# The order of attention units and output steps on TensorE, changed in a fused attention and FFN kernel

## The chip, the core and the metric

The kernel runs on one core of a Trainium2 chip. The metric is the device time of one execution in microseconds (us). Three runs of the kernel before gave 245.78, 246.03 and 246.22 us, so the median is 246.03 us. The execution that the profiler recorded took 245.78 us; its span, from the first to the last instruction of the program, is 244.0 us, so 1.78 us lie outside the span.

## The reference

Inputs are `q`, `k`, `v` of shape (4, 8, 768, 64), a small matrix `sort_net` (4, 8, 8, 8), and FFN weights `w_a`, `w_b` (512 x 1536) and `w_out` (1536 x 512). What is computed, cut to the core:

```python
P = sort_net
for _ in range(5):                       # rows, then columns, sum to one
    P = exp(P - P.max(-1)); P /= P.sum(-1); P /= P.sum(-2)
k_s = einsum('bhij,bhjcd->bhicd', P, k_b)    # k and v: 8 blocks of 96 rows, mixed by P
v_s = einsum('bhij,bhjcd->bhicd', P, v_b)
attn = softmax(q_b @ k_s.T / sqrt(64))       # within each block
x = concat_heads(attn @ v_s)                 # 3072 x 512
out = ((x @ w_a) * (x @ w_b)) @ w_out        # 3072 x 512
```

## The kernel before, in words

There are 4 batches with 8 heads each. Two heads are a **pair**; pairs are counted through, g = 0 to 15, four to a batch (`HP` = 4). The FFN of batch b runs on TensorE while the attention of batch b+1 is put in small pieces between the FFN's steps. Everything on TensorE (PE), GpSimd (POOL) and the SyncE queue (SP) runs in the order in which the Python code issues it (`manual_schedule`, L399). After the opening part, the order on VectorE (DVE) and ScalarE (ACT) is chosen by the scheduler.

**FFN steps.** `ffn_ab(b, m, t)` (L340) makes 128 of the 1536 hidden rows for half a batch: 4 matmuls for a and 4 for b (L332, 384 columns each, into the PSUM pool `psF`), a copy of a to SBUF by ACT (L352), and the product a*b by DVE into `hT` (L353). There are 24 such steps to a batch; for batch 0 the 12 steps with t = 0 run earlier, so 12 are left. `ffn_out(b, c)` (L368) makes 128 output rows: 12 accumulating matmuls of 512 columns (L377) into `po`, a copy to `o_sb` by ACT for even c and by DVE for odd c (`store`, L384), and the DMA to `out` on the SP queue. In the kernel before, `ffn_out` gives two steps of 6 matmuls each. There are 6 outputs c to a batch; I call them po0 to po5, and their halves po0a, po0b.

**Attention units.** A pair g of batch 1 to 3 has three units (L530):

- C, `c_(g)`: for g < 7 a transpose of q on TensorE (`turn_q`, L255); 12 matmuls that mix k and 12 that mix v (`stage_mix`, L274, L281), each into its own tile of `psA`; ACT copies k to `kT` in two copies and the second half of v to `vT`, DVE copies the first half of v. For g > 4 a DMA transpose on SP turns `vT` into `vs` (L292). From g = 6 a tiny POOL copy waits for `kT` (the gate, L539), and the loads of pair g+2 follow it.
- S, `s_(g)`: 16 matmuls of scores (`stage_scores`, L295, L302), 8 for each half of the blocks, each half into a tile of `psA`, and an exponential by ACT for each half (L307). Its weights are `kT`, its moving data the transposed q (`qT`). From g = 7 to 14 it also issues the next pair's q repack on POOL (`pair_q`, L244) and the DMA transpose on SP (`stage_q`, L250).
- O, `o_(g)`: 16 matmuls `o_ps` (L231) in two halves, each into a tile of `psA`; DVE takes reciprocals (L235) and scales into `xp` (L237); a DMA transpose on SP writes `xT` (L318), which the next batch's FFN reads.

The pool `psA` has two tiles of two PSUM banks, taken in turn. So the first half of an S or O needs the tile that the first half of the unit before it used to be read out, and the second half the other one. `psF` has four tiles of one bank. `kT`, `vT`, `vs` and `eT` have three buffers each, taken by g modulo 3.

**The order.** `paced` (L570) goes through the FFN's steps and puts in as many units after each as keeps the two in proportion. With C0 for the first pair of the coming batch, and "ab" for one `ffn_ab` step, the order during batch 0 is

```
ab C0 ab S0 ab ab C1 ab S1 ab ab C2 ab O0 ab ab S2 ab C3 ab po0a O1 po0b S3
po1a po1b O2 po2a O3 po2b po3a po3b po4a po4b po5a po5b
```

and during batches 1 and 2

```
ab C0 ab ab S0 ab ab ab C1 ab ab ab S1 ab ab C2 ab ab ab O0 ab ab ab S2 ab ab C3
ab ab ab O1 ab ab po0a S3 po0b po1a O2 po1b po2a po2b O3 po3a ... po5b
```

**The opening.** P is normalized, and the first half of batch 0's attention runs in pairs (`half_mix`, `half_scores`, `half_v`, `half_o`, `half_x`). Then five FFN accumulations are begun ahead of their last summand (`begun`, L488): three in `psF`, and two in the first halves of two `psA` tiles named `two` (L489). The steps ffn_ab(0,0,0), (0,1,0) and (0,2,0) add the last summand to them: the second step finishes begun 3, the third begun 4.

Of the kernel before, what the change touches and what calls it, by code (L numbers as in the profile page):

```python
# [9 lines left out]
FP32 = mybir.dt.float32  # L10
# [6 lines left out]
def _ap(t: bass.AP, extra_offset, pattern):  # L17
    return bass.AP(tensor=t.tensor, offset=t.offset + extra_offset,
                   ap=[list(p) for p in pattern])
# [3 lines left out]
def kernel(  # L23
# [11 lines left out]
    nc = tc.nc  # L35
    P = 128
    B, H, S, D = q.shape
# [3 lines left out]
    DMODEL = H * D  # L41
# [4 lines left out]
    NCH = S // P  # L46
    HP = H // 2
    KA = DMODEL // P
    KO = DFF // P
# [17 lines left out]
    psA = ctx.enter_context(tc.tile_pool(name="psA", bufs=2, space=PSUM))  # L67
    psF = ctx.enter_context(tc.tile_pool(name="psF", bufs=4, space=PSUM))
# [19 lines left out]
    def load_pair(b, hp):  # L88
        tiles = []
        for name, t in (("k2", k), ("v2", v), ("q2", q)):  # L90
            base = (b * H + 2 * hp) * S * D
            if b == 0 and name == "q2":
                continue
            to = ld.tile([P, 2, W], BF16, tag=name, name=name)
            nc.gpsimd.dma_start(out=to, in_=_ap(t, base, [[W, P], [S * D, 2], [1, W]]))  # L95
            tiles.append(to)
        loaded[b * HP + hp] = tiles
# [3 lines left out]
    w_out_sb = const.tile([P, KO, DMODEL], BF16, name="w_out_sb")  # L101
# [42 lines left out]
    def xT_of(b):  # L144
        if b not in xTs:
            xTs[b] = xtp.tile([P, KA, S], BF16, tag="xT", name="xT")
        return xTs[b]
# [12 lines left out]
    def copy(eng, out, in_):  # L160
        if eng == "act":
            nc.scalar.copy(out=out, in_=in_)  # L162
        else:
            nc.vector.tensor_copy(out=out, in_=in_)  # L164
# [79 lines left out]
    def pair_q(g):  # L244
        qc = qtp.tile([P, NCH, 2, D], BF16, tag="qc", name="qc", bufs=4)
        nc.gpsimd.tensor_copy(out=qc.rearrange("p c e d -> p e c d"),  # L246
                              in_=loaded[g][2].rearrange("p e (c d) -> p e c d", c=NCH))
        st[g, "qc"] = qc

    def stage_q(g):  # L250
        qT = qtp.tile([P, NCH, P], BF16, tag="qTf", name="qTf", bufs=4)
        nc.sync.dma_start_transpose(out=qT, in_=st[g, "qc"].rearrange("p c e d -> p (c e d)"))
        st[g, "qT"] = qT

    def turn_q(g, eng="dve"):  # L255
        q2 = loaded[g][2] if g >= HP else q_first[:, 2 * g:2 * g + 2]
        q_ps = psF.tile([P, NCH, P], BF16, tag="F", name="q_ps")
        for c in range(NCH):
            for e in range(2):
                nc.tensor.matmul(q_ps[e * D:(e + 1) * D, c, :],  # L260
                                 lhsT=q2[:, e, c * D:(c + 1) * D],
                                 rhs=ident, is_transpose=True)
        qT = qtp.tile([P, NCH, P], BF16, tag="qT", name="qT")
        copy(eng, qT, q_ps)
        st[g, "qT"] = qT

    def turn_v(g):
        vT, vs = vTs[g % NBUF], vss[g % NBUF]
        vs_ps = psF.tile([P, NB, P], BF16, tag="F", name="vs_ps")
        for i in range(NB):  # L270
            nc.tensor.matmul(vs_ps[:, i], lhsT=vT[:, i], rhs=ident, is_transpose=True)
        nc.vector.tensor_copy(out=vs[0:BLK, :, V0:V0 + P], in_=vs_ps[0:BLK])
# [43 lines left out]
    def to_xT(g):  # L316
        xT, xp = xT_of(g // HP), st[g, "xp"]
        nc.sync.dma_start_transpose(  # L318
            out=xT[:, g % HP, :].rearrange("p (i t) -> p i t", i=NB),
            in_=xp.rearrange("p i e d -> p (i e d)"))  # L320


    hTs = {}
# [32 lines left out]
    def ffn_last(b, c):  # L356
        hT = hTs[b]
        rows = out[b * S:(b + 1) * S, :].rearrange("(p c) n -> c p n", c=NCH)
        for n0, n1, eng, queue in ((0, 384, "act", nc.sync), (384, DMODEL, "dve", nc.scalar)):
            po = psF.tile([P, 512], FP32, tag="F", name="po")  # L360
            for m in range(KO):
                nc.tensor.matmul(po[:, 0:n1 - n0], lhsT=hT[:, m, c * P:(c + 1) * P],  # L362
                                 rhs=w_out_sb[:, m, n0:n1], start=(m == 0), stop=(m == KO - 1))
            o_sb = ffp.tile([P, 512], FP32, tag="o_sb", name="o_sb", bufs=3)
            copy(eng, o_sb[:, 0:n1 - n0], po[:, 0:n1 - n0])
            queue.dma_start(out=rows[c][:, n0:n1], in_=o_sb[:, 0:n1 - n0])

    def ffn_out(b, c):  # L368
        if b == B - 1 and c == NCH - 1:
            return [lambda: ffn_last(b, c)]  # L370
        held = {}

        def part(n):
            if n == 0:
                held["po"] = psF.tile([P, DMODEL], FP32, tag="F", name="po")
            for m in range(n * KO // 2, (n + 1) * KO // 2):
                nc.tensor.matmul(held["po"], lhsT=hTs[b][:, m, c * P:(c + 1) * P],  # L377
                                 rhs=w_out_sb[:, m, :], start=(m == 0), stop=(m == KO - 1))
            if n == 1:
                store(b, c, held["po"])  # L380

        return [lambda: part(0), lambda: part(1)]

    def store(b, c, po):  # L384
        o_sb = ffp.tile([P, DMODEL], FP32, tag="o_sb", name="o_sb", bufs=3)
        copy("act" if c % 2 == 0 else "dve", o_sb, po)
        if b == 0:
            h, u = divmod(c, 3)
            for c2 in range(2):
                nc.sync.dma_start(  # L390
                    out=_ap(out, (h * PH * NCH + 2 * u + c2) * DMODEL,
                            [[NCH * DMODEL, PH], [1, DMODEL]]),
                    in_=o_sb[c2 * PH:(c2 + 1) * PH])
        else:
            rows = out[b * S:(b + 1) * S, :].rearrange("(p c) n -> c p n", c=NCH)
            nc.sync.dma_start(out=rows[c], in_=o_sb)


    with tc.manual_schedule(engines={ET.PE, ET.Pool, ET.SP}):  # L399
        with tc.manual_schedule(engines={ET.Activation, ET.DVE}):  # L400
# [7 lines left out]
            for it in range(5):  # L408
# [15 lines left out]
                if it > 0:  # L424
                    nc.tensor.matmul(heat[0:NB, 1, 0:NB], lhsT=rsum, rhs=rsum,
                                     start=True, stop=True)
# [59 lines left out]
            half_x(0, 2, "act")  # L486
            half_o(0, 3)
            begun = [psF.tile([P, 512], FP32, tag="F", name="pf") for _ in range(3)]  # L488
            begun += [psA.tile([P, 2, 512], FP32, tag="A", name="two")[:, 0] for _ in range(2)]  # L489
            for n, (m, w_sb) in enumerate(((0, w_a_sb), (0, w_b_sb), (1, w_a_sb),  # L490
                                           (1, w_b_sb), (2, w_a_sb))):
                if n == 3:
# [37 lines left out]
        def units_full(b):  # L530
            g0, us = b * HP, []

            def c_(g):
                if g < 2 * HP - 1:
                    turn_q(g)
                stage_mix(g, "k", ("act",))
                stage_mix(g, "v", ("dve", "act"))
                if 2 * HP - 2 <= g < B * HP - 2:
                    nc.gpsimd.tensor_copy(out=gate, in_=kTs[g % NBUF][0:1, 0:1])  # L539
                    load_pair((g + 2) // HP, (g + 2) % HP)  # L540

            def s_(g):
                stage_scores(g)
                if g == HP:
                    turn_v(g)
                if g == HP + 1:
                    stage_q(2 * HP - 1)
                if 2 * HP <= g + 1 < B * HP:
                    pair_q(g + 1)
                    stage_q(g + 1)  # L550

            def o_(g):
                stage_o(g)
                to_xT(g)

            for u, n in ((c_, 0), (s_, 0), (c_, 1), (s_, 1), (c_, 2), (o_, 0), (s_, 2), (c_, 3),
                         (o_, 1), (s_, 3), (o_, 2), (o_, 3)):
                us.append(lambda u=u, g=g0 + n: u(g))
            return us

        def interleave(steps, units, spare, slow=0):
# [6 lines left out]
                    done += 1  # L568

        def paced(ab, po, units, spare):  # L570
            steps = ab + po
            total = len(steps) - 2 * spare
            done = 0
            for now, step in enumerate(steps, 1):
                step()
                while done < len(units) and done * total < now * len(units):
                    units[done]()
                    done += 1

        steps = [lambda: ffn_ab(0, 0, 0, begun[0:2]), lambda: ffn_ab(0, 1, 0, begun[2:4]),  # L580
                 lambda: ffn_ab(0, 2, 0, begun[4:5])]
# [3 lines left out]
        for b in range(B):  # L585
            ab = [lambda m=m, t=t, b=b: ffn_ab(b, m, t)
                  for m in range(KO) for t in range(2) if b > 0 or t == 1]
            po = [f for c in range(NCH) for f in ffn_out(b, c)]
            paced(ab, po, units_full(b + 1) if b + 1 < B else [], 3 if b == 0 else 2)


# [28 lines left out]
```

## Time and profile before

| what | value |
| --- | --- |
| three runs | 245.78, 246.03, 246.22 us; median 246.03 us |
| profiled execution | 245.78 us, span 244.0 us |
| TensorE matmul busy | 236.7 us, 97% of the span |
| VectorE, ScalarE, GpSimd busy | 109.6 us (45%), 104.6 us (43%), 60.6 us (25%) |
| matmuls of L332 (768) | start to start 162.5 ns in a run of them |
| matmuls of L377 (276) | start to start 216 ns in a run of them |
| TensorE clock granted | 1.00 throughout |
| batch 0 with its units, from C0 on | 45.50 to 85.04 us |
| batch 1 with its units | 85.04 to 139.56 us: 54.52 us |
| batch 2 with its units | 139.56 to 194.08 us: 54.52 us |
| batch 3, no units | 194.08 to 243.97 us |

The profile of one execution is read in views: the busy time of each engine, groups of instructions by source line with their mean duration, the chain of work that ended last, the timeline of instructions, and the time from a DMA's issue to its landing. A matmul's listed duration (326 ns for 384 columns) overlaps the next matmul, so the time that a row of matmuls takes is read from start to start. "Idle before, releaser" names what an engine waited for.

### The profile page before, as it was taken

How to read it: one execution, taken by the hardware profiler on the slowest of the kernel's cores; microseconds unless marked ns; L12 is line 12 of the kernel's file. 1: busy time of each engine (PE TensorE's matmuls, PEld its weight loads, DVE VectorE, ACT ScalarE, POOL GpSimd, SP SyncE). 2: the span in 40 equal slices, each digit the busy share in tenths (PEclk: the TensorE clock that was granted, in tenths of full speed). 3: DMA queues.
4: the chain of work that ended last, by engine and by line, in shares of the span. 5: the costliest groups of instructions: out<-in, count | busy, mean ns of one | idle time of the engine just before them, and what ended most of it. 6: DMA issues, size and time to landing. Idle time of an engine off the chain costs nothing.

```text
span 244.0 us, 5508 instructions
## 1 busy us (share of the span) xinstructions
PE 236.7 (97%) x2246; PEld 137.3 (56%) x2258; DVE 109.6 (45%) x259; ACT 104.6 (43%) x204; POOL 60.6 (25%) x87
## 2 busy tenths in 40 slices
PE   7889999999999999999999999999999999999995
PEld 2466666666545466666654466666654466665443
DVE  6774566555536144464625144454524243443110
ACT  3665864466730065646440065646430133333001
POOL 8875577613230043240500053200000000000000
PEclk9999999999999999999999999999999999999999
DMA  5999999958998659987783449924243310000122
GB/s 80 202 199 197 197 200 201 206 84 81 172 157 183 138 100 127 160 135 84 110 140 119 121 95 126 169 46 66 43 79 118 118 46 0 0 3 1 43 112 103
DMA packets 53129, 27.82 MB, mean 114 GB/s; under 512 B 29936, under 2 KB 50160, under 8 KB 53104
## 3 DMA queue, kind: packets, MB, share of 16 engines
q0 software_dynamic: 20944, 14.16, 40.6%
q1 hardware_dynamic: 32016, 13.25, 28.9%
q8 instruction: 17, 0.28, 0.5%
q14 instruction: 8, 0.07, 0.1%
q10 hardware_dynamic: 144, 0.07, 0.1%
HBM read 28.32 MB, written 6.29 MB: 142 GB/s over the span
## 4 chain that ended last, share of the span: by engine, by line
PE 94%; DVE 3%; issue 1%; ACT 1%
PE pf L332 52%; PE po L377 24%; PE mix L281 4%; PE o_ps L231 3%; PE sc L302 2%; PE heat L168 2%; PE mixh L180 2%; PE po L362 1%; PE vs_ps L208 1%; PE sc L195 1%; PE xt_ps L222 1%; PE q_ps L260 1%; PE two L332 1%; DVE xp L237 1%; DVE o_sb L164 0%
## 5 line engine op out<-in xcount | busy, mean ns | idle before, releaser
L353 DVE TENSOR_TENSOR hT<-a_sb,pf 128x384 bf16<-128x384 bf16 x95 | 52.6, 553 | 73.8 <-PE pf L332 47.1
L332 PE MATMUL pf<-xT,w_a_sb 128*128 128x384 bf16 x380 | 77.9, 326 | 0.0
L332 PE MATMUL pf<-xT,w_b_sb 128*128 128x384 bf16 x380 | 77.4, 326 | 0.0
L352 ACT CAST a_sb<-pf 128x384 bf16<-128x384 f32 x95 | 45.5, 479 | 60.9 <-PE pf L332 41.3
L377 PE MATMUL po<-w_out_sb,hT 128*128 128x512 bf16 x265 | 61.3, 379 | 0.6
L332 PEld LDWEIGHTS <-w_b_sb 128*128 128x128 bf16 x384 | 37.5, 98 | 24.6
L332 PEld LDWEIGHTS <-w_a_sb 128*128 128x128 bf16 x384 | 34.9, 98 | 22.3
L377 PEld LDWEIGHTS <-hT 128*128 128x128 bf16 x276 | 26.3, 98 | 30.0
L162 ACT COPY o_sb<-po 128x512 f32<-128x512 f32 (+1 forms) x13 | 7.5, 578 | 46.8 <-PE po L377 45.2
L164 DVE COPY o_sb<-po 128x512 f32<-128x512 f32 (+1 forms) x12 | 7.9, 655 | 35.2 <-PE po L377 26.3
L307 ACT ACTIVATE eT<-sc 96x768 bf16<-96x768 f32 x24 | 18.1, 802 | 6.8 <-PE sc L302 6.8
L539 POOL COPY gate<-kT 1x1 bf16<-1x1 bf16 x8 | 1.4, 179 | 76.1 <-ACT kT L162 76.1
L237 DVE TENSOR_TENSOR xp<-o_ps,rec 96x512 bf16<-96x512 f32 x24 | 15.9, 684 | 0.4
L162 ACT CAST kT<-mix 128x384 bf16<-128x384 f32 x24 | 10.3, 482 | 8.3 <-PE mix L281 8.3
L95 POOL DMA_DIRECT2D k<-in_k_dram x16 | 11.6, 724 | 5.1 <-PE pf L332 2.0
L95 POOL DMA_DIRECT2D v<-in_v_dram x16 | 11.5, 722 | 2.3 <-PE pf L332 0.7
L231 PEld LDWEIGHTS <-eT 96*128 96x128 bf16 x256 | 10.3, 97 | 3.2 <-DVE xp L237 0.6
L235 DVE RECIPROCAL rec<-o_ps 96x8 f32<-96x8 f32 x32 | 5.6, 189 | 14.0 <-PE o_ps L231 14.0
L231 PE MATMUL o_ps<-vs,eT 96*128 96x65 bf16 x256 | 11.3, 193 | 0.2 <-DVE xp L237 0.2
L246 POOL COPY qc<-q 128x768 bf16<-128x768 bf16 x9 | 7.6, 845 | 7.8 <-DMA q<-in_q_dram 7.8
L95 POOL DMA_DIRECT2D q<-in_q_dram x12 | 8.7, 722 | 1.6 <-DMA w_a_sb<-in_moe_w_a_dram 0.7
L168 PE MATMUL heat<-warm 128*128 128x512 bf16 x20 | 7.1, 497 | 1.4 <-DVE warm L77 1.3
(80 smaller groups left out, 155.4 us busy)
## 6 DMA issues: line engine op xcount, KB each, us to landing
out_dram<-o_sb SPq DMA_DIRECT2D x17, 256.0 KB, 2.0
k<-in_k_dram POOLq DMA_DIRECT2D x16, 192.0 KB, 5.3
v<-in_v_dram POOLq DMA_DIRECT2D x16, 192.0 KB, 6.9
q<-in_q_dram POOLq DMA_DIRECT2D x12, 192.0 KB, 7.1
w_a_sb<-in_moe_w_a_dram POOLq DMA_DIRECT2D x6, 256.0 KB, 10.5
w_b_sb<-in_moe_w_b_dram POOLq DMA_DIRECT2D x6, 256.0 KB, 10.2
w_out_sb<-in_moe_w_out_dram POOLq DMA_DIRECT2D x3, 512.0 KB, 10.0
out_dram<-o_sb SPq DMA_DIRECT2D x12, 128.0 KB, 2.4
```

The source lines that it names most:

```text
L95: nc.gpsimd.dma_start(out=to, in_=_ap(t, base, [[W, P], [S * D, 2], [1, W]]))
L162: nc.scalar.copy(out=out, in_=in_)
L164: nc.vector.tensor_copy(out=out, in_=in_)
L168: nc.tensor.matmul(ps[:, 0:cols], lhsT=warm[:, 0:P], rhs=warm[:, 0:cols], start=True, stop=True)
L231: nc.tensor.matmul(o_ps[:, e, i * (D + 1):(i + 1) * (D + 1)], lhsT=eT[:, hf, e, i * BLK:i * BLK + P], rhs=vs[0:BLK, i0 + i, V0 - 1 + e * ( ...
L237: nc.vector.tensor_tensor(out=_ap(xp, i0 * 2 * D, [[nxp * 2 * D, BLK], [D, 2], [2 * D, NBH], [1, D]]), in0=_ap(o_ps, 1, [[1024, BLK], [511 ...
L281: nc.tensor.matmul(mix[e * D:(e + 1) * D, c // 3, c % 3 * P:(c % 3 + 1) * P], lhsT=src2[:, e, c * D:(c + 1) * D], rhs=s_all[:, 2 * g + e], ...
L307: nc.scalar.activation(out=eT[:, hf, :, 0:HB], in_=sc[0:BLK, :, 0:HB], func=AF.Exp, scale=float(scale))
L332: nc.tensor.matmul(pf[:, 0:HW], lhsT=w_sb[:, kc, m * P:(m + 1) * P], rhs=x_cols(b, kc, t), start=(kc == 0), stop=(kc == KA - 1))
L352: nc.scalar.copy(out=a_sb, in_=pf[:, 0:HW])
L353: nc.vector.tensor_mul(out=hT[:, m, t * HW:(t + 1) * HW], in0=a_sb, in1=ab[1][:, 0:HW])
L377: nc.tensor.matmul(held["po"], lhsT=hTs[b][:, m, c * P:(c + 1) * P], rhs=w_out_sb[:, m, :], start=(m == 0), stop=(m == KO - 1))
```

## The change

The diff, cut to its core:

```diff
     def ffn_out(b, c):
-        held = {}
-        def part(n):
-            if n == 0:
-                held["po"] = psF.tile([P, DMODEL], FP32, tag="F", name="po")
-            for m in range(n * KO // 2, (n + 1) * KO // 2):
-                nc.tensor.matmul(held["po"], ...
-            if n == 1:
-                store(b, c, held["po"])
-        return [lambda: part(0), lambda: part(1)]
+        po = psF.tile([P, DMODEL], FP32, tag="F", name="po")
+        for m in range(KO):
+            nc.tensor.matmul(po, ...
...
-            begun += [psA.tile([P, 2, 512], FP32, tag="A", name="two")[:, 0] for _ in range(2)]
+            two = psA.tile([P, 2, 512], FP32, tag="A", name="two")
+            begun += [two[:, 0], two[:, 1]]
...
             def s_(g):
-                if 2 * HP <= g + 1 < B * HP:
-                    pair_q(g + 1)
-                    stage_q(g + 1)
             def o_(g):
                 stage_o(g)
                 to_xT(g)
+                if 2 * HP <= g + 2 < B * HP:
+                    pair_q(g + 2)
+                    stage_q(g + 2)
-            for u, n in ((c_, 0), (s_, 0), (c_, 1), (s_, 1), (c_, 2), (o_, 0), (s_, 2), (c_, 3),
-                         (o_, 1), (s_, 3), (o_, 2), (o_, 3)):
-                us.append(lambda u=u, g=g0 + n: u(g))
+            for n in range(HP + 1):
+                if n < HP:
+                    us.append(lambda g=g0 + n: c_(g))
+                    us.append(lambda g=g0 + n: s_(g))
+                if n > 0:
+                    us.append(lambda g=g0 + n - 1: o_(g))
...
         def paced(ab, po, units, spare):
-            steps = ab + po
-            total = len(steps) - 2 * spare
+            steps = [(1, f) for f in ab] + [(2, f) for f in po]
+            total = sum(t for t, f in steps) - 2 * spare
```

No instruction is added or dropped. The units come in the order C0 S0 C1 S1 O0 C2 S2 O1 C3 S3 O2 O3, an output step is one piece of 12 matmuls that counts double in the pacing, q's repack and transpose for pair g+2 are issued in the unit O of pair g, and begun 3 and 4 share one `psA` tile. Written out, the order during batch 0 becomes

```
ab C0 ab S0 ab ab C1 ab S1 ab ab O0 ab C2 ab ab S2 ab O1 ab po0 C3 S3
po1 O2 po2 O3 po3 po4 po5
```

and during batches 1 and 2

```
ab C0 ab ab S0 ab ab ab C1 ab ab ab S1 ab ab O0 ab ab ab C2 ab ab ab S2 ab ab O1
ab ab ab C3 ab ab po0 S3 po1 O2 po2 O3 po3 po4 po5
```

On ACT the scheduler puts the copy of po0 to `o_sb` in batch 0 ahead of the three copies of C3. On SP the DMA transpose of `vs` for C3 follows the stores of po0, as it follows the `xT` of O1.

More of the change, by code (lines that the diff above doesn't have):

```diff
@@ L369, in ffn_out @@
         if b == B - 1 and c == NCH - 1:
-            return [lambda: ffn_last(b, c)]
-        held = {}
-        def part(n):
-            if n == 0:
-                held["po"] = psF.tile([P, DMODEL], FP32, tag="F", name="po")
-            for m in range(n * KO // 2, (n + 1) * KO // 2):
-                nc.tensor.matmul(held["po"], lhsT=hTs[b][:, m, c * P:(c + 1) * P],
-                                 rhs=w_out_sb[:, m, :], start=(m == 0), stop=(m == KO - 1))
-            if n == 1:
-                store(b, c, held["po"])
-        return [lambda: part(0), lambda: part(1)]
-    def store(b, c, po):
+            ffn_last(b, c)
+            return
+        hT = hTs[b]
+        po = psF.tile([P, DMODEL], FP32, tag="F", name="po")
+        for m in range(KO):
+            nc.tensor.matmul(po, lhsT=hT[:, m, c * P:(c + 1) * P], rhs=w_out_sb[:, m, :],
+                             start=(m == 0), stop=(m == KO - 1))
         o_sb = ffp.tile([P, DMODEL], FP32, tag="o_sb", name="o_sb", bufs=3)
@@ L570, in paced @@
         def paced(ab, po, units, spare):
-            steps = ab + po
-            total = len(steps) - 2 * spare
-            done = 0
-            for now, step in enumerate(steps, 1):
+            steps = [(1, f) for f in ab] + [(2, f) for f in po]
+            total = sum(t for t, f in steps) - 2 * spare
+            now = done = 0
+            for t, step in steps:
                 step()
+                now += t
                 while done < len(units) and done * total < now * len(units):
@@ L587 @@
                   for m in range(KO) for t in range(2) if b > 0 or t == 1]
-            po = [f for c in range(NCH) for f in ffn_out(b, c)]
+            po = [lambda c=c, b=b: ffn_out(b, c) for c in range(NCH)]
             paced(ab, po, units_full(b + 1) if b + 1 < B else [], 3 if b == 0 else 2)
```

## The prediction

> **What bounds the kernel now.** I read the busy time first, then the chain of work that ended last. Of the page:
>
> ```profile
> PE 236.7 (97%) x2246; PEld 137.3 (56%) x2258; DVE 109.6 (45%) x259; ACT 104.6 (43%) x204; POOL 60.6 (25%) x87
> PE 94%; DVE 3%; issue 1%; ACT 1%
> ```
>
> TensorE is the bound, and no other engine comes near half. A listed matmul overlaps its successor, so 97% does not say that TensorE loses only 3%; I therefore lay the starts of the matmuls side by side. One step of 8 matmuls takes 1.30 us (162.5 ns each), an output 2.59 us (12 x 216 ns), a unit C 0.79 (with turn_q 0.36 more), S 0.446, O 0.493 us. In front of every C and every S one more 0.10 us stands (24 matmuls take 4.00 us before a C or S, 3.91 before an O). With these, batch 1 comes to 24 x 1.30 + 6 x 2.59 + 4 x (0.79 + 0.446 + 0.493) + 8 x 0.10 = 54.5 us, and 54.52 is what batches 1 and 2 each take. So there TensorE waits for nothing, and the old order has nothing left to lose there. What time before loses to order is seen in batch 0. From the timeline around its end (start, length, engine, line):
>
> ```profile
> 70.08 0.20 PEld L302 LDWEIGHTS <-kT 64*128 64x128 bf16 x8 [0.42 <-DVE rec L235]
> 70.46 0.20 PEld L302 LDWEIGHTS <-kT 64*128 64x128 bf16 x8 [0.18 <-DVE xp L237]
> ...
> 75.12 0.30 PEld L231 LDWEIGHTS <-eT 96*128 96x128 bf16 x8 [0.32 <-DVE xp L237]
> 75.71 0.30 PEld L231 LDWEIGHTS <-eT 96*128 96x128 bf16 x8 [0.30 <-DVE xp L237]
> ```
>
> S3 and O3 wait for DVE to read out the unit half an output earlier, because the two psA tiles are in use. S3 takes 0.655 us for 0.446, O3 0.849 for 0.493: 0.21 and 0.36 lost.
>
> **The change, term by term.** The instructions are the same, so the sum consists of TensorE waits that go and that come.
>
> **1. The shared tile `two`.** In the program built from the changed kernel, the last matmul of begun 4 (step (0,2,0)) has a wait for DVE that the old one lacks: the product of step (0,1,0) reads the other half of the same tile. The timeline of before at that place:
>
> ```profile
> 26.20 0.34 PE L332 MATMUL two<-xT,w_a_sb 128*128 128x384 bf16 x1
> ...
> 26.27 0.55 DVE L353 TENSOR_TENSOR hT<-a_sb,two 128x384 bf16<-128x384 bf16 x1 [0.77 <-PE mixh L180]
> ...
> 26.38 0.81 PE L332 MATMUL pf<-xT,w_b_sb 128*128 128x384 bf16 x4
> ```
>
> The matmul starts at 26.20, the DVE product ends at 26.82, and nothing ahead of that product changes (the orders on ACT and DVE are the same up to there). TensorE runs in order, and 0.05 us pass from a DVE end to the start that waits for it (75.66 to 75.71): it starts at 26.88, **+0.68 us**. The ACT copy behind it began at 26.92 and moves by 0.3 to 0.7, into idle time. Nothing later takes the loss back: from 27 us to C0 no block of matmuls stands more than 0.17 us over its nominal time, so no fixed event is being waited for. Bounds: 0.62 (no latency) to 0.75.
>
> [...]
>
> **2. S3 directly behind C3 in batch 0.** po0 counts double, so C3 and S3 both fall due after it. S3 needs kT, and its second half the psA tile of the v mix. How long these copies take, the old C3 shows:
>
> ```profile
> 64.80 0.53 PE L281 MATMUL mix<-s_all,k 128*64 128x128 bf16 x12
> 65.36 0.86 ACT L162 CAST kT<-mix 128x384 bf16<-128x384 f32 x2 [0.16 <-PE mix L281]
> 66.29 0.48 ACT L162 CAST vT<-mix 128x384 bf16<-128x384 f32 x1
> 66.80 1.24 SPq L292 DMA_TRANSPOSE vs<-vT  x1
> ...
> 70.19 0.59 ACT L162 COPY o_sb<-po 128x512 f32<-128x512 f32 x1 [3.03 <-PE po L377]
> ```
>
> Count from the first matmul of C3. kT could start at +0.56, but ACT now has the copy of po0 ahead of it: that begins 0.11 after po0 (70.08 to 70.19) and lasts 0.48 to 0.59, so kT starts at +0.59 to 0.70, ends 0.86 later, and vT ends 0.55 after that, at +2.00 to 2.11. The second half of S3 starts 0.05 later and takes 0.22: C3 and S3 end at +2.27 to 2.38, against 0.79 + 0.446 = 1.24 without a wait. **+1.1 us** (1.03 to 1.14, up to 1.25 if the weight loads behind the waits are exposed). Behind S3 on TensorE stands all else, so this is paid in full.
>
> **3. Waits that go.** S3's tiles now come from C3 (term 2) and no longer from O1, and O3 has O2 and the whole po2 (0.49 + 2.59 us) in front of it, where DVE needs 2.3 from O2's start (73.34 to 75.66): **-0.21 and -0.36**. One of the steps of 0.10 goes, since S3 follows C3 at once: **-0.10**. Bounds: -0.67, and -0.57 if that step stays.
>
> **4. O3's `vs`.** What is late next. The vs of C3 goes through an SP transpose that starts when vT is copied, at +2.1 (issue at 66.80 in before is +2.00). O3 starts at 2.35 + 2.60 (po1) + 0.49 (O2) + 2.59 (po2) = +8.03. So O3 waits if issue to landing takes over 5.9 us. In before the old O3 came 8.3 us after the issue, and had 1.26 us to spare. The page has
>
> ```profile
> vs<-vT SPq DMA_TRANSPOSE x11, 5.8
> ```
>
> and the seven that ran beside loads of k, v and q took 4.85, 5.47, 5.81, 6.09, 6.52, 7.07 and 7.42 us; 7.07 is this very pair's. The gate on kT still releases the loads of pair 9 just ahead of it. Beyond 5.94 these seven give 0, 0, 0, 0.15, 0.58, 1.13, 1.48: mean 0.48. I take **+0.5 us**, bounds 0 and 1.5.
>
> [...]
>
> **5. What I cost at nothing.** O3's xT: xp is ready 2.25 us after O3's start, SP still has q's transpose and po2's stores until about 2.85, and xT rows of batch 0 took 3.48 to 5.59 to land: at most +8.4, needed at +8.76 (0.49 + 3 x 2.59 + 0.49 into the first step). The cover is 0.3 us at worst; without it, some 0.5. Pair q's transpose for S2 of batches 1 and 2: xT was issued 2.29 and the q transpose 3.60 us after O0's start (107.03, 109.32, 110.63); S2 starts 0.49 + 4.00 + 0.79 + 4.00 = 9.28 after it, so a landing of up to 5.68 us is hidden; of nine rows two (6.09, 6.58) exceed that, both beside loads that are not in flight at the new place. Price: 0 to 0.9 at each of the two places, taken as 0. On POOL the q repack moves behind the next pair's three load issues (0.72 each), whose q landed long before. O0 and O1 earlier in all batches: their exponentials (1.88 us after S) are two steps back. O1 only one step (1.31 us) after S2 in batch 0: its second half starts 2.0 after S2, the second exponential ends at 1.88; hidden by 0.1. Batches 1 and 2: **0**. Batch 3 and the end: unchanged.
>
> **Sum:** 0.68 + 1.1 - 0.67 + 0.5 = **+1.6 us**. The profiled execution (245.78, span 244.0) becomes 247.4; it lies 0.25 below the median of the runs, so I forecast a median of 246.03 + 1.6 = **247.6 us**.
>
> **Rivals.**
>
> - *vs lands late in full.* With 7.42 us, as in batch 2's first pair, O3 waits 1.5: sum 2.6, **248.6**. For it: the same pair had 7.07, and po0's stores now lie just ahead. Against: four of seven rows are at or near no wait.
> - *The wait on `two` is not felt*, if the DVE product ends sooner or ACT feeds it earlier: sum 0.9, **247.0**. Against: its inputs are unchanged.
> - *Not slower.* One mechanism: the 0.10 us before each C and S is a wait that the order makes, not a cost of the kind of matmul. The new order then sheds it at 16 places in batches 1 and 2, -1.6, and the sum is 0: **246.0**, or less if batch 0 sheds it too (0.7 more, 245.3). It decides from 16 places on. Against: it stands before C and S alike, after ab and po, two or three steps from the last unit, and never before O.
> - *A transfer of batches 1 and 2 becomes late* (q's transpose, twice 0.9 at most): sum up to 3.4, **249.4**. Against: no loads in flight there.
>
> **Chances.** Forecast 0.57 (247.1 to 248.1), vs late 0.17, `two` not felt 0.12, not slower 0.05, late transfer 0.09. The unknown costs bound the sum at 0.62 + 1.03 - 0.67 + 0 = 1.0 and 0.75 + 1.25 - 0.57 + 1.5 = 2.9; with the first three cases (0.86) and some 0.1 of spread at the ends the range is 246.8 to 249.1. About 0.2% (0.5 us) is what a measurement of this kernel can tell from no change. Faster 0.03 and same 0.02 come from the fourth case; the lower end of the third adds 0.02 to same; slower 0.93.
>
> **What the changed profile would show.** Term 1: the last matmul on `two` starts 0.6 to 0.7 later, released by DVE. Term 2: ACT's copy of kT releases S3's weights near 71.5 us, with the vT copy behind. Term 3: S3 and O3 no longer wait on xp. Term 4: O3 waits for the transposed vs, or not. Batches 1 and 2 at 54.5 us each. I am wrong if these two stages change length, if the matmul on `two` is not held, or if a TensorE wait stands where I have none.

## The result and the profile after

The changed kernel has a median of **247.19 us** (six runs, 246.59 to 247.84) against 246.00 us (six runs, 245.48 to 246.53) for the kernel before: a ratio of **1.0048, 95% interval 1.0026 to 1.0069**, so 0.6 to 1.7 us slower. The profiled execution took 247.31 us, with a span of 245.5 us against 244.0.

The page's busy time and chain, in the same lines as those shown of before, hardly differ:

```profile
PE 236.9 (96%) x2246; PEld 137.5 (56%) x2258; DVE 109.1 (44%) x259; ACT 104.4 (43%) x204; POOL 60.6 (25%) x87
PE 94%; DVE 3%; issue 1%; ACT 1%
```

They cannot show the loss, since it consists of a few waits of under 1 us each, at two places. The busy times by stretch do. The first column is the stretch, the second its length, the rest busy times, clock and DMA:

```profile
21.96:46.69 24.73, 24.02 (x306) 15.07 (x303) 13.35 (x30) 13.38 (x27) 15.43 (x19) 1.00 1.36 200
46.69:86.63 39.94, 38.85 (x426) 22.92 (x429) 18.09 (x38) 17.63 (x34) 9.12 (x12) 1.00 0.80 130
86.63:141.16 54.53, 54.37 (x487) 31.43 (x488) 23.41 (x47) 23.81 (x47) 12.70 (x20) 1.00 0.73 130
141.16:195.69 54.53, 54.37 (x487) 31.37 (x489) 23.39 (x47) 23.80 (x47) 6.33 (x10) 1.00 0.48 93
```

| stretch, from the starts of TensorE's matmuls | before | changed | difference | predicted |
| --- | --- | --- | --- | --- |
| start to the first matmul of L332 | 21.45 | 21.96 | +0.51 | 0 |
| from there to C0 of batch 0 | 24.06 | 24.73 | +0.67 | +0.68 |
| batch 0 with its units | 39.54 | 39.94 | +0.40 | +0.93 (0.43 without O3's wait) |
| batch 1 | 54.52 | 54.53 | +0.01 | 0 |
| batch 2 | 54.52 | 54.53 | +0.01 | 0 |
| batch 3 to the end | 49.89 | 49.86 | -0.03 | 0 |

The opening's 0.51 us is no part of the change. Its code is the same in every kernel here, and in the twelve profiled executions of this study it takes 21.43 to 22.47 us. What is left, 1.06 us, is what the change costs in this execution.

The wait on the shared tile, from the timeline of the changed kernel (start, length, engine, line; in brackets the idle time and what ended it):

```profile
26.79 0.56 DVE L353 TENSOR_TENSOR hT<-a_sb,two 128x384 bf16<-128x384 bf16 x1 [0.77 <-PE mixh L180]
...
27.39 0.32 PE L332 MATMUL two<-xT,w_a_sb 128*128 128x384 bf16 x1 [0.61 <-DVE hT L353]
```

The matmul starts 0.04 us after the product ends. The 24 small matmuls ahead of it and this wait take 1.18 us; before they took 0.50.

C3 and S3 in the timeline of the changed kernel:

```profile
70.37 0.53 PE L281 MATMUL mix<-s_all,k 128*64 128x128 bf16 x12
70.48 0.59 ACT L162 COPY o_sb<-po 128x512 f32<-128x512 f32 x1 [2.71 <-PE po L375]
...
70.96 0.87 ACT L162 CAST kT<-mix 128x384 bf16<-128x384 f32 x2
...
71.87 0.48 ACT L162 CAST vT<-mix 128x384 bf16<-128x384 f32 x1
...
71.88 0.34 PE L302 MATMUL sc<-qTf,kT 64*128 64x96 bf16 x8 [0.65 <-ACT kT L162]
...
72.40 1.29 SPq L292 DMA_TRANSPOSE vs<-vT  x1
72.40 0.35 PE L302 MATMUL sc<-qTf,kT 64*128 64x96 bf16 x8 [0.17 <-ACT vT L162]
...
78.36 0.66 PE L231 MATMUL o_ps<-vs,eT 96*128 96x65 bf16 x16
```

The first half of S3 is released by kT, the second by the vT copy. S3's last matmul is followed by po1, whose first matmul is missing from the records; 0.216 us before the first recorded one (72.90) gives 72.68, so C3 and S3 took 2.32 us, 1.08 more than their own 1.24. The last line is O3. It has no wait: its vs landed at 78.17, 5.77 us after the issue, and O3 was due at 78.36. That is close: where O3 does wait for vs below, it starts 0.13 to 0.14 us after the landing (77.73 to 77.87 with halved outputs), so here it had some 0.06 us to spare. The wait of the old S3 and O3 for DVE's read-out is gone.

### The profile page after: what moved, and what is told of

Its sections match the earlier page's. It is cut to its first block, busy times and chain, and to the rows that moved or that the text cites. A ratio compares the mean times of both kernels' runs of the same rounds, so it can differ in the third digit from the quotient of the medians.

```text
span 245.5 us, 5508 instructions
## 1 busy us (share of the span) xinstructions
PE 236.9 (96%) x2246; PEld 137.5 (56%) x2258; DVE 109.1 (44%) x259; ACT 104.4 (43%) x204; POOL 60.6 (25%) x87
## 4 chain that ended last, share of the span: by engine, by line
PE 94%; DVE 3%; issue 1%; ACT 1%
PE pf L332 51%; PE po L375 24%; PE mix L281 4%; PE o_ps L231 3%; PE heat L168 2%; PE sc L302 2%; PE mixh L180 2%; PE po L362 1%; PE vs_ps L208 1%; PE sc L195 1%; PE xt_ps L222 1%; PE q_ps L260 1%; PE two L332 1%; PE mixh L168 0%; ACT qT L162 0%
## 5 line engine op out<-in xcount | busy, mean ns | idle before, releaser
L332 PE MATMUL pf<-xT,w_a_sb 128*128 128x384 bf16 x380 | 77.8, 326 | 0.0
L332 PE MATMUL pf<-xT,w_b_sb 128*128 128x384 bf16 x380 | 77.4, 326 | 0.0
L375 PE MATMUL po<-w_out_sb,hT 128*128 128x512 bf16 x265 | 60.5, 379 | 0.7 <-issue 0.2
L332 PEld LDWEIGHTS <-w_b_sb 128*128 128x128 bf16 x384 | 37.5, 98 | 25.2 <-issue 0.6
L332 PEld LDWEIGHTS <-w_a_sb 128*128 128x128 bf16 x384 | 34.9, 98 | 22.2
L168 PE MATMUL heat<-warm 128*128 128x512 bf16 x20 | 7.6, 527 | 1.4 <-DVE warm L77 1.3
L164 DVE CAST vT<-mix 128x384 bf16<-128x384 f32 x12 | 6.7, 558 | 3.9 <-PE mix L281 3.8
```

The source lines that it names most:

```text
L168: nc.tensor.matmul(ps[:, 0:cols], lhsT=warm[:, 0:P], rhs=warm[:, 0:cols], start=True, stop=True)
L332: nc.tensor.matmul(pf[:, 0:HW], lhsT=w_sb[:, kc, m * P:(m + 1) * P], rhs=x_cols(b, kc, t), start=(kc == 0), stop=(kc == KA - 1))
L375: nc.tensor.matmul(po, lhsT=hT[:, m, c * P:(c + 1) * P], rhs=w_out_sb[:, m, :], start=(m == 0), stop=(m == KO - 1))
```

## The experiments

Each kernel ran beside the kernel before on the same chip; medians of the latter were 245.73 to 245.78 us there. Lengths of stretches are from one profiled execution of each.

### The two tiles apart again, in the changed kernel

```diff
-            two = psA.tile([P, 2, 512], FP32, tag="A", name="two")
-            begun += [two[:, 0], two[:, 1]]
+            begun += [psA.tile([P, 2, 512], FP32, tag="A", name="two")[:, 0] for _ in range(2)]
```

> The changed kernel with begun 3 and 4 in two psA tiles again, as before; all else as changed. Theory (the shared tile makes TensorE wait for DVE's product, 0.66 to 0.68 us): the 24 small mix matmuls ahead of the last matmul on two take 0.50 us instead of 1.18, the median falls from 247.2 to about 246.5, 0.4 above the kernel before; batch 0 from C0 on stays at 39.9. Rival (the wait is taken up by slack later): the block shrinks, the time stays at 247.2.

The timeline of this kernel:

```profile
26.46 0.34 PE L332 MATMUL two<-xT,w_a_sb 128*128 128x384 bf16 x1
```

The wait is gone, and the stretch from the first matmul of L332 to C0 is 24.06 us, as before the change. The median is 246.84 us, ratio 1.0047 (1.0032 to 1.0063): 0.8 to 1.5 us over the kernel before, where 0.4 was expected. The profiled execution shows two parts of the rest: O3 waited 0.21 us for vs (landing 6.04 us after its issue; batch 0 took 40.14), and the opening took 21.70 us. Taking the unchanged stretches from the six spans (244.9 to 245.6 us) leaves 21.9 to 22.6 us for the opening and O3's wait together. How much of this is O3's wait in the executions that have no profile stays open, and so the 0.67 us is shown by the stretch and not by this median.

### The shared tile alone, in the kernel before

```diff
-            begun += [psA.tile([P, 2, 512], FP32, tag="A", name="two")[:, 0] for _ in range(2)]
+            two = psA.tile([P, 2, 512], FP32, tag="A", name="two")
+            begun += [two[:, 0], two[:, 1]]
```

> The kernel before with begun 3 and 4 in the two halves of one psA tile, nothing else changed. Theory: +0.66 us, median about 246.7; the 24 small mix matmuls ahead of the last matmul on two take 1.18 us instead of 0.50; batch 0 from C0 on stays at 39.5. Rival (the wait is taken up by slack later): 246.0.

```profile
27.13 0.32 PE L332 MATMUL two<-xT,w_a_sb 128*128 128x384 bf16 x1 [0.61 <-DVE hT L353]
```

This line of its timeline is the wait again. The stretch to C0 is 24.72 us (24.06 before), batch 0 stays at 39.54, batches 1 and 2 at 54.52. Median 246.81 us, ratio 1.0040 (1.0024 to 1.0055), 0.6 to 1.35 us: the 0.66 lies in it, and in the profiled execution the opening took 0.25 more (21.70 us). So this edit costs its price alone, and nothing later takes it back.

### The new order of units with halved outputs

```diff
-        po = psF.tile([P, DMODEL], FP32, tag="F", name="po")
-        for m in range(KO):
+        def part(n):
...
+        return [lambda: part(0), lambda: part(1)]
...
-            steps = [(1, f) for f in ab] + [(2, f) for f in po]
+            steps = ab + po
```

> The changed kernel with its order of units, but outputs given in halves and paced as before: po0a C3 po0b S3 po1a po1b O2 po2a O3 po2b. Theory (S3 waits only because nothing lies between C3 and S3; O3 waits for the transposed vs if that lands over 5.0 us after its issue): S3's wait of 1.08 goes, a step of 0.10 comes, O3 waits 0.8 for vs at a landing of 5.8 us: batch 0 from C0 on 39.76 instead of 39.94, median about 247.0. Rival (O3's only limit is DVE's read-out of O2, 0.36 as in the kernel before): 39.3, median about 246.55.

S3, now behind half an output, takes 0.456 us: it waits no more. O3 does, in the timeline of this kernel:

```profile
77.87 0.65 PE L231 MATMUL o_ps<-vs,eT 96*128 96x65 bf16 x16 [1.60 <-DMA vs<-vT]
```

vs landed 6.67 us after its issue (71.06 to 77.73), and po2a and the wait together took 3.06 us for 1.30. Batch 0 is 40.74 us, not 39.76: the transfer holds O3, as the theory has it and the rival has not, but it took 0.9 us longer than I supposed. The median of all seven executions is 247.61 us; six of them, at a mean clock of 0.998 or more, took 246.49 to 248.17 (ratio 1.0060, 1.0039 to 1.0081), and one took 250.57 at 0.993. In four profiled executions of these kernels this landing took 5.77, 6.04, 6.21 and 6.67 us; if it differs as much between executions of one kernel, O3's wait also spreads their times, an estimate that no profile here shows.

### C3 one step earlier

```diff
+                placed(ab, po, units_full(1), (1, 2, 4, 5, 7, 8, 10, 11, 12, 13, 14, 15))
```

The numbers are the FFN step of batch 0 after which each unit comes; only C3's differs from the changed kernel (12 for 13).

> The changed kernel with one unit moved by one step: C3 of batch 0 ahead of po0 instead of behind it, so that po0 lies between C3 and S3. Theory: S3's wait of 1.08 goes, a step of 0.10 comes, and C3's v mix waits about 0.3 for DVE to read out O1: batch 0 from C0 on 39.25 instead of 39.94, median about 246.5. Rival (C3 and S3 are held by something other than their neighbourhood, or the wait moves to C3 in full): 39.9, median 247.2.

The timeline of this kernel:

```profile
67.63 1.29 DVE L237 TENSOR_TENSOR xp<-o_ps,rec 96x512 bf16<-96x512 f32 x2
...
68.46 0.53 PE L281 MATMUL mix<-s_all,k 128*64 128x128 bf16 x12
...
69.06 0.53 PE L281 MATMUL mix<-s_all,v 128*64 128x128 bf16 x12
...
72.21 0.52 PE L302 MATMUL sc<-qTf,kT 64*128 64x96 bf16 x16
```

S3 (72.21, 0.447 us) and O3 wait no more. C3 now waits for DVE to read out O1, at both tiles: the profile names no releaser, but DVE's second read ends at 68.92, 0.14 us ahead of the first v matmul. The step ahead of C3 and the wait take 1.575 us for 1.302, and C3 1.057 us for 0.793: 0.27, of which 0.10 stands before every C, and 0.26, where I had a wait of 0.3 in all. Batch 0 is 39.42 us (39.25 expected), the median 246.31, ratio 1.0020 (1.0004 to 1.0036). C3's neighbourhood is what cost the 1.08.

### po0 copied by DVE

```diff
-        copy("act" if c % 2 == 0 else "dve", o_sb, po)
+        copy("act" if c % 2 == 0 and (b, c) != (0, 0) else "dve", o_sb, po)
```

> The changed kernel with po0 of batch 0 copied to o_sb by DVE instead of ACT, so that nothing stands ahead of the kT copies on ACT. Theory (S3 waits for the length of C3's own copies; the copy of po0 only adds 0.03 to 0.14): C3 and S3 together 2.2 to 2.3 us instead of 2.32, median 247.1. Rival (ACT's backlog makes the wait): 0.5 less, median 246.7.

C3 and S3 take 2.31 us (2.32 in the changed kernel): the copy of po0 ahead of kT on ACT costs nothing, and S3 waits for C3's own chain of copies. The median is 247.28 us, ratio 1.0060 (1.0042 to 1.0078). Batch 0 took 40.41, because in this execution O3 waited 0.48 us for vs, which landed after 6.21 (from start to start; the line below starts later and shows less, since six of the 16 matmul records of O3 are not in it):

```profile
78.30 0.47 PE L231 MATMUL o_ps<-vs,eT 96*128 96x65 bf16 x10 [0.32 <-DMA vs<-vT]
```

### kT's second copy by DVE

```diff
-                stage_mix(g, "k", ("act",))
+                stage_mix(g, "k", ("act", "dve") if g == 2 * HP - 1 else ("act",))
```

> The changed kernel with the second copy of C3's kT in batch 0 made by DVE instead of ACT. The scheduler then puts the exponential of S3's first half ahead of the vT copy on ACT. Theory (S3's first half waits for kT, its second half for the psA tile of v, so for the last vT copy): the first half of S3 starts 1.15 us after C3's first matmul instead of 1.51, but the second half waits for exponential and vT copy: C3 and S3 together take 3.0 us instead of 2.32, median about 247.9. Rival (kT alone holds S3): 1.6 us together, median 246.5.

The timeline of this kernel, and its busy times in two stretches:

```profile
71.58 0.34 PE L302 MATMUL sc<-qTf,kT 64*128 64x96 bf16 x8 [0.86 <-DVE kT L164]
...
72.82 0.35 PE L302 MATMUL sc<-qTf,kT 64*128 64x96 bf16 x8 [0.90 <-ACT eT L307]
```

```profile
73.30:77.40 4.10, 4.07 (x12) 1.51 (x12) 0.00 (x0) 0.71 (x1) 1.26 (x2) 0.58 1.17 149
77.40:80.00 2.60, 2.60 (x27) 1.46 (x26) 2.12 (x5) 0.00 (x0) 0.82 (x1) 1.00 0.73 137
```

C3 and S3 take 3.25 us (69.86 to 73.11), near the 3.0 of the theory and far from the 1.6 of the rival, so kT's copies alone do not hold S3. But they come to it otherwise than the theory had it. The first half started 1.72 us after C3 and not 1.15, since DVE began its kT copy only when ACT's had ended (70.93), and ended it at 71.52. The second half started at 72.82, 0.05 us after the exponential of the first half ended (72.77) and before the vT copy did (73.14). So here the exponential, which stands ahead of vT, released it, as the profile names it; in the changed kernel the second half started 0.05 us after vT's copy and before that exponential ended. Why the two differ stays open. Then comes what neither side had: po1 took 4.28 us instead of 2.59 at a granted clock of 0.58. The median is 248.83 us, ratio 1.0122 (1.0103 to 1.0141); the three executions at a mean clock of 0.999 or 1.000 took 247.88 to 248.49, the three at 0.993 took 249.16 to 249.50.

### O3 directly behind O2

```diff
+                placed(ab, po, units_full(1), (1, 2, 4, 5, 7, 8, 10, 11, 13, 13, 14, 14))
```

> The changed kernel with O3 of batch 0 directly behind O2, ahead of po2. Theory (vs of C3 lands about 5.8 us after its issue, so 2.4 us after O3 could now start): O3 is held for about 2.4 us by that transfer, batch 0 from C0 on 42.4, median about 249.7. Rival (only DVE's read-out of O2's two tiles holds it, its first tile free 1.25 us and its second 1.9 us after): 41.9, median 249.1, and the release comes from DVE.

```profile
77.97 0.65 PE L231 MATMUL o_ps<-vs,eT 96*128 96x65 bf16 x16 [2.31 <-DMA vs<-vT]
```

Batch 0 takes 42.40 us, and the release comes from the transfer (72.12 to 77.83, 5.71 us), at both points as the theory had it. The median, 251.23 us (ratio 1.0194, 1.0157 to 1.0231), is 1.5 over what was expected. Two of six executions took 249.5 at a mean clock of 0.999, four took 251.1 to 251.7 at 0.992 or 0.993: the clock again.

### The loads of pair 9 held back

```diff
-                    load_pair((g + 2) // HP, (g + 2) % HP)
+                    if g != 2 * HP - 1:
+                        load_pair((g + 2) // HP, (g + 2) % HP)
...
+                    if g == 2 * HP - 2:
+                        nc.gpsimd.tensor_copy(out=gate, in_=st[g, "xp"][0:1, 0, 0, 0:1])
+                        load_pair((g + 3) // HP, (g + 3) % HP)
```

> The changed kernel with the loads of pair 9 (k, v, q) held back by a POOL copy of O2's xp, so that they are issued near 77.8 us instead of 72 to 74, behind the transposed vs of C3 instead of beside it. Theory (vs takes 5.5 to 6.7 us to land because it shares the DMA engines with these loads, and O3 waits for it in some executions): vs of C3 lands about 3.0 us after its issue, O3 never waits, batch 0 from C0 on 39.94 us, median about 0.3 under the changed kernel, 246.9. Rival (the landing time is the transpose's own at this place): vs lands after 5.5 us or more, batch 0 between 39.94 and 40.4, median 247.2.

vs landed 3.06 us after its issue (71.88 to 74.94), batch 0 took 39.94 us, and O3 did not wait. Beside the loads the changed kernel's took 5.77 us, so here the loads made the difference. But the time rose: median 248.71 us, ratio 1.0121 (1.0106 to 1.0135). The loads now lay beside O3's xT, which took 6.41 us to land (81.46 to 87.87), where the changed kernel's took 2.84. The timeline of this kernel at the start of batch 1:

```profile
87.91 0.32 PE L332 MATMUL pf<-xT,w_a_sb 128*128 128x384 bf16 x1 [1.15 <-DMA xT<-xp]
```

Batch 1 took 55.83 us for 54.53. The wait that was taken away at one transfer came back at the next.

### The late issue of q's transpose, in the kernel before

```diff
             def s_(g):
-                if 2 * HP <= g + 1 < B * HP:
-                    pair_q(g + 1)
-                    stage_q(g + 1)
             def o_(g):
+                if 2 * HP <= g + 2 < B * HP:
+                    pair_q(g + 2)
+                    stage_q(g + 2)
```

> The kernel before with the q repack and q transpose for pair g+2 issued in unit O of pair g, nothing else changed. Theory (the transposed q lands before S needs it): 0, median 246.0, batches 1 and 2 at 54.52 us each. Rival (q's transpose is late for S2 of batches 1 and 2): S2 waits up to 0.9 us in each, up to 247.8.

Both were far off: the median is 259.22 us, ratio 1.0524 (1.0478 to 1.0571), batches 1 and 2 take 60.88 and 61.33 us. I had reckoned with the distance from O0 to S2 in the changed order (9.28 us). In the old order C2 already stands ahead of O0, so S2 starts 0.49 + 4.00 = 4.5 us after O0, and the transpose, issued 3.6 us after O0, must land first. The timeline of this kernel, and two stretches around S3:

```profile
114.44 0.52 PE L302 MATMUL sc<-qTf,kT 64*128 64x96 bf16 x16 [2.08 <-DMA qTf<-qc]
```

```profile
125.40:129.30 3.90, 1.39 (x6) 0.50 (x6) 0.55 (x1) 0.01 (x1) 0.83 (x1) 1.00 0.90 115
129.30:134.00 4.70, 4.69 (x28) 1.95 (x29) 0.00 (x0) 2.09 (x3) 0.00 (x0) 0.64 0.00 2
```

S2 waits 2.1 us and S3 2.5 in batch 1, 3.0 and 2.0 in batch 2. After S3 of batch 1 the next twelve matmuls of an output take 4.28 us instead of 2.60, in a stretch at a clock of 0.64. So the change's new place for q's transpose costs nothing together with its new order of units, while in the old order it cost 13 us. The new order with q's transpose in its old place was not run.

### A version without these waits

```diff
+                placed(ab, po, units_full(1), (1, 2, 4, 5, 7, 8, 9, 10, 12, 13, 14, 15))
```

This is the changed kernel with two tiles for begun 3 and 4 and this placing in batch 0: S2, O1 and C3 one step earlier each.

> Two psA tiles for begun 3 and 4, and in batch 0 the units placed by hand so that neither C3 and S3 nor O2 and O3 stand close: ab C0 ab S0 ab ab C1 ab S1 ab ab O0 ab C2 ab S2 ab O1 ab ab C3 po0 S3 po1 O2 po2 O3 po3 po4 po5; batches 1 and 2 as in the changed kernel. Theory (the waits named are all there are): batch 0 from C0 on 38.96 us (39.54 before, 39.94 changed), median about 245.45, 0.55 under the kernel before. Rival (a wait is only moved to C3, S2 or O1, whose neighbours are now closer): 39.5 or more, median 246.0 or more.

```profile
67.39 0.53 PE L281 MATMUL mix<-s_all,k 128*64 128x128 bf16 x12
...
70.88 0.51 PE L302 MATMUL sc<-qTf,kT 64*128 64x96 bf16 x16
...
73.93 0.66 PE L231 MATMUL o_ps<-vs,eT 96*128 96x65 bf16 x16
...
77.02 0.66 PE L231 MATMUL o_ps<-vs,eT 96*128 96x65 bf16 x16
```

In its timeline C3, S3, O2 and O3 carry no wait in brackets. Batch 0 takes 38.98 us (38.96 expected), the stretch to C0 24.06. The median is **245.20 us** over 12 runs, ratio **0.9975 (0.9965 to 0.9986)**: 0.3 to 0.9 us under the kernel before and the fastest here. To within 0.02 us, the waits named are all there were in batch 0.

## Why the prediction was right, and where it was off

- **What bounds it, and batches 1 and 2 at 0.** Right. They take 54.53 us each in the changed kernel, 54.52 before. The 0.10 us ahead of each C and S is unmoved, so the rivals "not slower" and "a transfer of batches 1 and 2 becomes late" fall.
- **Term 1, the shared tile: +0.68.** Right: +0.67 in the changed kernel, +0.66 with this edit alone, 0 with it undone. The trace shows the wait (0.61 us, released by DVE's product); no run here shows whether it was needed.
- **Term 2, S3 behind C3: +1.1.** Right: 2.32 us for C3 and S3, predicted 2.27 to 2.38. The two runs on the copies agree: with po0's copy elsewhere it stays (2.31), so the first bound counted, not ACT's queue; with the exponential put ahead of vT it grows (3.25), though that run does not show vT to be what holds the second half.
- **Term 3, waits that go: -0.67.** Right. Terms 2 and 3 make +0.43 of batch 0's +0.40.
- **Term 4, O3's vs: +0.5.** This is the term that was mis-sized, and most of the error: 0.5 where the profiled execution has 0, which is all but 0.05 of what 1.06 falls short of 1.6. Its mechanism stands: an earlier O3 waits for vs in full (2.31 us), a vs alone lands in 3.06 us. But at the place itself the wait was 0 in the profiled execution, 0.21 and 0.48 in two others with the same order, at landings of 5.77, 6.04 and 6.21 us. I had averaged seven landings from 4.85 to 7.42; nearly all of the mean came from the three longest. (An eighth that ran beside such loads, 6.22 us from 150.91, was left out; with it the mean is 0.45.) That the wait was nothing in the profiled execution, by 0.06 us, is luck. With these three waits the mean is 0.23, and the sum 0.67 + 0.40 + 0.23 = 1.3 us against the measured 1.19 (0.6 to 1.7). po1 and po2 cover the landing; po2 took 2.59 us, 216 ns a matmul, as reckoned.
- **What was costed at nothing** cost nothing: no wait at S2 or S3 of batches 1 and 2, at O1, or at the start of batch 1. That these covers are real was shown where they are gone: 2.0 to 3.0 us each at S2 and S3 of the kernel with q's transpose late, 1.30 us for xT with the loads beside it. One cover was reckoned too large: O3's xT was issued 4.03 us after O3's start (82.39), not 2.85, as q's transpose and two stores of po2 held the SP queue until 82.30. It landed in 2.84 us and was in time; at the 5.59 us of the worst row of before it would have been some 0.9 us late.

Of the rivals, "vs lands late in full" was not met in the profiled execution or by the median, and "`two` is not felt" is refuted by the trace.

## What to carry to other kernels

When one engine is busy throughout, lay its instructions side by side from start to start: a change of order is then worth the waits that it makes and removes at single places, and each can be priced from the copies or transfers that stand between two neighbours. Here two accumulators in one tile shared the tile's wait (0.66 and 0.67 us), though neither touches the other's half. A hand-written order carries its transfers with it: moving an issue, a unit or a load alone turned a free transfer into 1.3 to 3.0 us of waiting here, and the same transfer landed in 3.06 us alone and in 5.77 us beside three loads.

## What the runs showed of the hardware

**The clock fell after short waits.** TensorE's granted clock dropped for some 3.4 us after waits shorter than that: after 0.86 and 0.90 us within 1.7 us (S3 with kT's copy on DVE; clock 0.58 from 73.30 to 77.40) and after 2.5 and 3.0 us (q's transpose late; 0.64 from 129.30 to 134.00 after the 2.5). The length is worked out: matmuls of 512 columns came 0.43 us apart, twice the 0.216 of elsewhere, and at half rate both stretches lose their share in about 3.4 us. It cost 1.7 us each time (4.28 us for 2.59 or 2.60), as much as the two waits of the first case together. Waits of 2.1 us (q's transpose late, at 114.44) and 2.31 us (O3 behind O2, in the profiled execution) were not followed by a drop, and four other executions of that last kernel had one, to judge by their mean clock (0.992 and 0.993, against 0.999): the wait alone does not decide it.

What goes with the drops in these traces is how busy TensorE was, by the profile's busy time, in one stretch of 3.41 us. The drops of the kernel with q's transpose late run from 129.77 to 133.19 and from 177.56 to 180.97, 14 lengths of 3.41 us later, and the one of the kernel with kT's copy on DVE from 73.66 to 77.08. Cut into such stretches, the two kernels with a drop read (busy times of PE, PEld, DVE, ACT and POOL, then the clock):

```profile
70.25:73.66 3.41, 1.49 (x36) 1.05 (x32) 1.02 (x2) 2.31 (x5) 2.26 (x4) 1.00 0.47 85
73.66:77.08 3.42, 3.42 (x10) 1.21 (x8) 0.00 (x0) 0.35 (x1) 0.90 (x2) 0.50 1.28 163
...
112.71:116.12 3.41, 1.68 (x24) 1.16 (x25) 0.31 (x1) 1.30 (x2) 0.00 (x0) 1.00 0.31 58
116.12:119.53 3.41, 3.41 (x42) 2.09 (x40) 1.67 (x3) 2.36 (x7) 0.38 (x2) 1.00 0.00 0
126.36:129.77 3.41, 0.95 (x20) 0.42 (x18) 0.00 (x0) 0.08 (x1) 0.83 (x1) 1.00 0.78 89
129.77:133.19 3.42, 3.42 (x12) 1.19 (x10) 0.00 (x0) 2.01 (x3) 0.00 (x0) 0.50 0.00 0
```

The first two lines are of the kernel with kT's copy on DVE, the others of the one with q's transpose late. A drop followed where TensorE was busy for 1.49, 0.95 and 1.31 us (174.15 to 177.56, ahead of the drop at 177.56), and none where it was busy for 1.68 us (the wait of 2.1 us) or 1.85 us (O3 behind O2, 76.41 to 79.82, counted back 50 lengths from that run's next change of the clock at 247.07, so an estimate; its wait of 2.31 us fell partly into the stretch before). These are five stretches, and no run moved a wait from the one group to the other with all else equal: that the busy time decides it is not shown. One drop to half the clock for 3.41 us lowers the mean over 248 us by 0.007: the profiled execution with one drop has 0.993, the one with two 0.987. That the other executions at 0.993 had one such drop each is an estimate from this.

**The transpose of vs within SBUF landed in 3.0 to 3.1 us alone** (3.06 in the kernel with the loads held back, 3.04 and 3.05 in the kernel before, from 158.85 and 171.20) **and in 5.5 to 7.1 us beside three loads** of 192 KB each that were issued within 1.2 us of it (seven in the changed kernel, 5.52 to 7.06); where two of the loads came 1.2 and 1.9 us after it, it took 4.40 us (from 90.03 there). One took 9.35 us, from 92.73 in the kernel with the loads held back, with stores and a second set of loads beside it. With no load beside it but a transfer or two of the program's instructions (queues q8 and q14 in the DMA view), as for the changed kernel's at 164.85 and 177.19, it took 4.3 and 4.7 us.
